# A Fourier mixing layer and an MLP on one core: first batch in units of four frequencies by whole filter rows, its last stages in residue order and mostly inside the MLP

## The chip, the cores and the metric

The kernel runs on one core of a Trainium2 chip. The metric is the device time of one execution in microseconds (us). A run's time is a little longer than the span of its profile (784.55 against 782.8 us for the kernel before), because the span counts from the first to the last instruction. Nearly all numbers below are read from profiles, so they are spans and moments within them; whole times and ratios are marked as such. In the profiles PE is TensorE, which does the matmuls and transposes; DVE (VectorE), ACT (ScalarE) and POOL (GpSimd) do the copies and products; SP issues DMAs. PSUM is the memory that the matmuls here write to and that DVE and ACT copy from.

## The reference

```python
def _attn_ref(x, filt_r, filt_i):            # x: 8 x 3008 x 256
    X = np.fft.rfft(x, axis=1)
    Y = X * (filt_r + 1j * filt_i)[None]     # filters: 1505 x 256
    return np.fft.irfft(Y, n=x.shape[1], axis=1).astype(np.float32)

def _moe_ref(x, w_in, w_out, beta):          # x: 24064 x 256, w_in: 256 x 2048
    h = x @ w_in
    g = h * (1.0 / (1.0 + np.exp(-beta * h)))
    return (g @ w_out).astype(np.float32)    # w_out: 2048 x 256
```

The MLP takes the 8 x 3008 tokens of the mixing layer. It is by far the larger part: 752 steps of two matmuls of 512 columns (into `hps`) and four of 256 columns (into `acc`).

## The kernel before

The length 3008 is split as 47 x 64. The transform is four stages of matmuls: two forward (s1, s2), a product with the filter, two backward (s3, s4). The tables of sines are made on the chip. Batch 0 is done ahead of the MLP, in what I call the head. Batches 1 to 7 are done inside the MLP's steps, as TensorE, DVE and ACT allow, by way of two DRAM scratch arrays.

The head as it was (cuts marked `# ...`). The filters are loaded in six parts of 8 frequencies by 128 channels, that is in rows of 512 bytes. `fr` comes into the lower 64 partitions and `fi` into the upper; POOL copies each to the other half (`spread`). DVE makes two products from each part:

```python
parts = ((0, KH, 0, E2), (KH, 2 * KH, 0, E2), (2 * KH, NK, 0, E2), (0, KH, E2, D), ...)
def load_filters(k0, k1, d0, d1):
    for filt, dst, p0 in ((filt_r, fr_sb, 0), (filt_i, fi_sb, M)):
        for q0, off, sg in ((p0, k0, 1), (p0 + H, N1 - k0, -1)):
            src = AP(filt.tensor, filt.offset + off * D + d0, [[N1 * D, H], [sg * D, n], [1, d1 - d0]])
            nc.sync.dma_start(dst[q0 : q0 + H, k0:k1, d0:d1], src)
def spread(n):
    nc.gpsimd.tensor_copy(fr_sb[M:, ks, ds], fr_sb[:M, ks, ds])
    nc.gpsimd.tensor_copy(fi_sb[:M, ks, ds], fi_sb[M:, ks, ds])
def s2_0(n):
    # ... eight matmuls into ps
    for c, filt in enumerate((fr_sb, fi_sb)):
        nc.vector.tensor_tensor(r_t[:], ps[:], filt[:, ks, ds], ALU.mult)      # pq_t
# POOL's order:
spread(0); spread(1); spread(2); spread(3)      # ...
spread(4)
nc.gpsimd.dma_start(win_sb[:], moe_w_in.rearrange("(dc p) f -> p dc f", p=P))
spread(5)
for g in range(4):
    load_x(1, g)                                 # x of batch 1
```

The end of the head: the result `zT` is turned by 64 transposes into `zz0` (z_turn), and 64 residue matmuls (f_0 and s4_0) make `y`. Much of the first half of the channels is done while the second half's products are still being made:

```python
s3_0(3); s2_0(5); f_0(0, 0, True); z_turn(0, 2, True); f_0(0, 1, True); z_turn(0, 3, True)
s3_0(4); s3_0(5, (False, True)); z_turn(1, 0, False, True); z_turn(1, 1, True, True)  # ...
f_0(0, 7, False); s4_0(1, 3, False)
```

The MLP loop, the plan of batch 1 (the numbers are MLP steps) and the last block. The `lags` say how many steps later the four output matmuls of a step come:

```python
for s in range(NSTEP + 4):
    # two matmuls hps <- win_sb, y ; ACT: gT <- silu(hps)
    for fn, a in plan.get(s, ()): fn(*a)        # stages of the next batch
    # four matmuls acc <- gT, wout_sb of an earlier step; DVE copies acc to ost at a block's end
s1_steps(1, range(16), [o + i // 2 for i in range(16)], False, range(1, 16, 2))
s23_steps(1, [o + r for r in (19, 21, 23, 26, 28, 30, 34, 36, 39, 41, 44, 46)], 5, 1)
lags[NBLK - 1] = (2, 2, 5, 7)
```

## Time and profile before

| | before |
|---|---|
| time, median of 3 runs | 784.76 us (784.7 to 784.91) |
| span of the profile | 782.8 us |
| first hps matmul of the MLP | 41.54 us |
| last filter product ends | 32.77 us |
| start of first hps to start of last matmul | 736.9 us |
| start of last matmul to the end | 4.29 us |

First the windows view of the kernel before. Its columns are the stretch, its length, then busy time and number of instructions of PE, PE's weight loads, DVE, ACT and POOL, the granted clock, the DMA share and GB/s.

```profile
core 0: us, PE busy (x) PEld busy (x) DVE busy (x) ACT busy (x) POOL busy (x), PEclk, DMA share, GB/s
0.00:41.54 41.54, 32.41 (x438) 25.09 (x440) 32.89 (x56) 30.32 (x43) 27.59 (x46) 1.00 1.04 203
41.54:778.50 736.96, 731.53 (x5540) 519.83 (x5632) 404.50 (x626) 528.18 (x781) 124.02 (x114) 1.00 0.39 108
```

In the head no engine is full and the DMA engines are (share 1.04). In the MLP TensorE is busy nearly all the time, and its starts follow at a fixed pitch: 109 ns for 256 columns, 216 ns for 512, 55 ns for a transpose of 128, about 42 ns for 94.

Next POOL's and DVE's timelines of the kernel before, at the end of the filter work (start, busy time, engine, line, what).

```profile
25.51 1.04 POOL L468 COPY fi_sb<-fi_sb 64x1024 f32<-64x1024 f32 x1
26.50 0.84 POOL L513 DMA_DIRECT2D win_sb<-in_moe_w_in_dram  x1
27.39 1.03 POOL L467 COPY fr_sb<-fr_sb 64x1024 f32<-64x1024 f32 x1
28.48 1.04 POOL L468 COPY fi_sb<-fi_sb 64x1024 f32<-64x1024 f32 x1
...
31.55 1.21 DVE L433 TENSOR_TENSOR pq_t<-sps,fi_sb 128x1024 bf16<-128x1024 f32 x1
```

The last filter copy starts at 28.48 us and does not wait; the product that needs it runs from 31.55. There are two microseconds of slack between them. The w_in load is issued at 26.50 us.

Last the chain of waits of the kernel before, in order of time, around the end of the head.

```profile
32.93 1.02 ACT zz L112
33.95 0.92 ACT zT L112
...
40.00 2.25 DVE y L116 x3
42.26 0.05 issue
42.30 0.39 PE hps L756
```

### The profile page before, as it was taken

The page shows a single profiled execution, that of the slowest core. Times are in us where ns is not written, and L with a number is a line of the kernel's source. Part 1 is how long each engine was busy: PE and PEld are TensorE (multiplying, and loading weights), DVE is VectorE, ACT ScalarE, POOL GpSimd, SP SyncE. Part 2 cuts the span into 40 slices and gives each one's busy share as a digit, 9 for nine tenths or more (in the row PEclk, how much of TensorE's full clock was granted, in tenths as well). Part 3 has the DMA queues.
Part 4 walks back from the last instruction along what each step waited for, and adds up shares of the span by engine and source line. Part 5 has one row for each costly group of instructions (what it writes and reads, how often), then busy time and mean ns, then how long its engine had stood idle before and what let it go on. Part 6 is the DMA issues. An engine that isn't in the chain of part 4 may idle for free.

```text
span 782.8 us, 15166 instructions
## 1 busy us (share of the span) xinstructions
PE 764.2 (98%) x5978; PEld 544.9 (70%) x6071; DVE 438.1 (56%) x682; ACT 558.5 (71%) x824; POOL 151.6 (19%) x160
## 2 busy tenths in 40 slices
PE   8799999999999999999999999999999999999997
PEld 5666767766677667866678666786667776676665
DVE  7747654776556665566655675466655666320101
ACT  6788867676667766776667776677666777777776
POOL 6714300322012120122101222012200222000000
PEclk9999999999999999999999999999999999999999
DMA  9966675234822349033580416612164211500101
GB/s 178 230 190 138 145 201 167 68 88 120 238 75 64 98 114 260 32 84 99 121 236 29 126 56 158 198 58 85 49 188 118 66 48 49 155 28 28 55 28 55
DMA packets 89835, 88.51 MB, mean 113 GB/s; under 512 B 5708, under 2 KB 80972, under 8 KB 89764
## 3 DMA queue, kind: packets, MB, share of 16 engines
q1 hardware_dynamic: 85588, 73.81, 31.8%
q0 software_dynamic: 4032, 13.60, 10.5%
q8 instruction: 47, 0.77, 0.4%
q14 instruction: 24, 0.20, 0.1%
q10 hardware_dynamic: 144, 0.13, 0.1%
HBM read 54.47 MB, written 46.66 MB: 129 GB/s over the span
## 4 chain that ended last, share of the span: by engine, by line
PE 94%; ACT 2%; issue 1%; DVE 0%; ACTq 0%
PE acc L774 43%; PE hps L756 39%; PE ps L572 3%; PE ps L639 3%; PE ps L617 3%; PE ps L588 2%; ACT zT L112 1%; ACT zz L112 1%; ACT t3s L291 0%; DVE y L116 0%; PE sps L396 0%; PE sps L444 0%; PE tps L396 0%; ACT a L112 0%; PE sps L428 0%
## 5 line engine op out<-in xcount | busy, mean ns | idle before, releaser
L765 ACT ACTIVATE gT<-hps,beta_sb 128x512 bf16<-128x512 f32 x752 | 515.8, 687 | 208.3 <-PE hps L756 187.2
L774 PE MATMUL acc<-wout_sb,gT 128*128 128x256 bf16 x3008 | 453.2, 272 | 2.5
L756 PE MATMUL hps<-y,win_sb 128*128 128x512 bf16 (+7 forms) x1636 | 428.3, 350 | 1.1 <-ACT y L112 0.6
L774 PEld LDWEIGHTS <-gT 128*128 128x128 bf16 x3008 | 287.6, 98 | 125.9 <-issue 1.2
L607 POOL TENSOR_TENSOR yh<-a_t,b_t 128x512 bf16<-128x512 f32 x84 | 106.4, 1266 | 420.4 <-DVE b_t L606 419.5
L756 PEld LDWEIGHTS <-win_sb 128*128 128x128 bf16 x1728 | 164.9, 98 | 25.6 <-issue 0.7
L114 DVE COPY ost<-acc 128x512 f32<-128x512 f32 (+1 forms) x94 | 60.0, 679 | 147.1 <-PE acc L774 147.1
L114 DVE CAST a<-ps 96x512 bf16<-96x512 f32 x104 | 70.9, 685 | 52.1 <-PE ps L572 48.0
L602 DVE TENSOR_TENSOR a_t<-ps,fr_sb 128x512 f32<-128x512 f32 x84 | 58.1, 692 | 70.0 <-PE ps L588 69.5
L116 DVE TENSOR_SCALAR y<-ps 128x376 bf16<-128x376 f32 x104 | 56.0, 548 | 59.3 <-PE ps L639 59.1
L603 DVE SCALAR_TENSOR_TENSOR b_t<-ps,fi_sb 64x512 f32<-64x512 f32 x84 | 58.2, 692 | 1.1
L606 DVE TENSOR_TENSOR b_t<-ps,fi_sb 64x512 f32<-64x512 f32 x84 | 57.4, 683 | 1.1
L114 DVE CAST z<-ps 128x512 bf16<-128x512 f32 x72 | 49.3, 684 | 1.7 <-PE ps L617 0.8
L639 PEld LDWEIGHTS <-zz 96*128 96x128 bf16 x448 | 29.8, 98 | 22.9
L572 PE MATMUL ps<-xg,t 94*96 94x512 bf16 x112 | 41.5, 381 | 0.6
L639 PE MATMUL ps<-t,zz 96*128 96x94 bf16 x448 | 34.7, 205 | 0.8
L617 PE MATMUL ps<-yh,t 128*128 128x256 bf16 x168 | 32.1, 273 | 0.6
L588 PE MATMUL ps<-a,t 128*128 128x256 bf16 x168 | 32.1, 273 | 0.3
L617 PEld LDWEIGHTS <-t 128*128 128x128 bf16 x168 | 16.3, 98 | 17.7
L588 PEld LDWEIGHTS <-t 128*128 128x128 bf16 x168 | 16.1, 98 | 15.2
L171 POOL DMA_DIRECT2D xg<-in_x_dram x24 | 12.4, 519 | 56.5 <-PE ps L572 56.5
L572 PEld LDWEIGHTS <-t 94*96 94x96 bf16 x112 | 13.8, 123 | 10.3
(103 smaller groups left out, 185.9 us busy)
## 6 DMA issues: line engine op xcount, KB each, us to landing
out_dram<-ost SPq DMA_DIRECT2D x46, 512.0 KB, 3.0
d<-a SPq DMA_DIRECT2D x28, 384.0 KB, 4.7
a<-d SPq DMA_DIRECT2D x28, 384.0 KB, 5.1
d<-z SPq DMA_DIRECT2D x28, 384.0 KB, 3.7
zz<-d SPq DMA_DIRECT2D x28, 384.0 KB, 6.1
xg<-in_x_dram POOLq DMA_DIRECT2D x24, 384.0 KB, 6.2
ws<-in_moe_w_out_dram SPq DMA_DIRECT2D x4, 512.0 KB, 6.0
fr_sb<-in_filt_r_dram SPq DMA_DIRECT2D x12, 128.0 KB, 4.6
```

The source lines that it names most:

```text
L114: nc.vector.tensor_copy(dst, src)
L572: nc.tensor.matmul(ps[:KP], lhsT=t1[:], rhs=xg[b, g][:NP, jj : jj + 2, :], start=True, stop=True)
L588: nc.tensor.matmul(ps[:, e, :], lhsT=t2[:, k0 + e, :], rhs=st["a2", b, g][:, kk + e, :], start=True, stop=True,)
L602: nc.vector.tensor_tensor(a_t[:], ps[:], fr_sb[:, ks, :], ALU.mult)
L603: nc.vector.scalar_tensor_tensor(b_t[:M], ps[M:], -1.0, fi_sb[M:, ks, :], ALU.mult, ALU.mult)
L606: nc.vector.tensor_tensor(b_t[M:], ps[:M], fi_sb[M:, ks, :], ALU.mult)
L607: nc.gpsimd.tensor_tensor(yh[:], a_t[:], b_t[:], ALU.add)
L617: nc.tensor.matmul(ps[:, e, :], lhsT=t3[:, 2 * i + e, :], rhs=yh[:, e, :], start=True, stop=True)
L639: nc.tensor.matmul(ps[:, e, :NP], lhsT=zz[:, j0 % JG + e, dc * P : (dc + 1) * P], rhs=t4[:], start=True, stop=True,)
L756: nc.tensor.matmul(hps[:, pos - t0 : pos - t0 + ln], lhsT=win_sb[:, dc, fb * P : (fb + 1) * P], rhs=ys[b][:, dc, n0 : n0 + ln], start=(dc ...
L765: nc.scalar.activation(gT[:], hps[:], ACT.Silu, scale=beta_sb[:, fb : fb + 1])
L774: nc.tensor.matmul(acc_of(i, tb)[:, tb % 2, :], lhsT=blk[i * NFB + fb][:, tb * P : (tb + 1) * P], rhs=wout_sb[:, fb, :], start=(fb == 0 an ...
```

## The change

The intent is to shorten the head. The head is worked in six units of four frequencies by all 256 channels, so the filters come in whole rows of 1 KB, and where four rows lie together, in 4 KB. The sign of the second table goes into the product, so that two half tables less have to be made. The tokens of batch 0 are ordered by residue, so that the first MLP block needs only one quarter of the transposes and residue matmuls; the other three quarters, 48 transposes and 48 matmuls, go into MLP steps 0 to 23. The core of the diff:

```diff
-    parts = ((0, KH, 0, E2), (KH, 2 * KH, 0, E2), ...)
+    def load_filters(k0, k1):        # rows of [1, D] instead of [1, d1 - d0]
...
+        nc.vector.scalar_tensor_tensor(
+            pq[u, 1][:], ps[:], rot[:], fi_sb[:, ks, :], ALU.mult, ALU.mult
+        )
...
-    spread(3)                        # POOL's order before: spread 0 to 4, w_in, spread 5, x
+    for u in range(3):
+        spread(u)
+    nc.gpsimd.dma_start(win_sb[:], moe_w_in.rearrange("(dc p) f -> p dc f", p=P))
+    spread(3)
+    spread(4)
+    load_x(1, 0)
+    spread(5)
+    for g in range(1, 4):
+        load_x(1, g)
...
+    s5 = [lps.tile([P, KU, P], F32, name="lp", tag="lp") for _ in range(NDC)]
+    s3_0(NUN - 1, s5)                # the last unit, then only quarter 0:
+    # ... z_evac, z_turn(0, ...), f4(0, ...), f4_head, f4_tail
...
+            at(0, z_late, 1, 0)
+            at(1, z_late, 1, 1)
+            s1_steps(1, range(16), [(2 * i + 1) // 3 for i in range(16)], False, (1, 4, 7, 10, 13))
+            for i, r in enumerate((11, 11, 12, 13)):
+                at(r, f_late, 1, i // 2, i % 2)
+            # ... quarters 2 and 3 in steps 13 to 23
-            s23_steps(1, [o + r for r in (19, 21, 23, 26, 28, 30, 34, 36, 39, 41, 44, 46)], 5, 1)
+            s23_steps(1, [o + r for r in (21, 23, 26, 28, 30, 32, 35, 37, 39, 41, 44, 46)], 5, 1)
...
-    lags[NBLK - 1] = (2, 2, 5, 7)
+    lags[NBLK - 1] = (2, 2, 4, 6)
```

## The prediction

> **What bounds the kernel now.** The span is 782.8 us. The timeline shows two regimes. From the first MLP matmul (hps, 41.54 us) on, TensorE hardly waits after two steps: the windows show 99.3 us busy in each 100, and starts follow at a fixed pitch: 109 ns for 256 columns, 216 for 512, 55 for a 128-column transpose, about 42 for 94 columns. (The Trainium skill, "TensorE: Matmul & The Clock Gate", section "Wait — 56ns, not 53.3ns?", gives 56 ns between 128-column matmuls; this trace agrees, with 55.) Before 41.54 us TensorE has slack: busy 7.2 to 8.0 of 10 us between 10 and 40 us. There the pace is set by a chain: POOL's filter copies (2.1 us a unit, first at 13.76 us, waiting for the filter DMA), twelve DVE filter products (1.22 us each, one per 1.14 us, 16.5 to 32.8 us, nearly gapless), then last unit, transposes to zz, 64 residue matmuls and their copies by ACT and DVE, 32.8 to 42.3 us.
>
> **What the change does.** It adds no matmul work; it cuts the 8.8 us tail between the last product and the first MLP step. Only the first quarter (16 transposes, 16 residue matmuls) stays ahead of the MLP; 48 transposes and 48 matmuls go into MLP steps 0 to 23. The filters arrive in 1 KB packets instead of 512 B; the packets' times (about 48 against 41 ns, so about 340 against 220 GB/s) put the six units earlier.
>
> **Costing the head.** POOL: spread from about 13.2 us, six units at 2.2 us plus 1.4 us of DMA issues: last unit ready at 27.7. DVE: first product at about 15.8 (16.5 before), so the last ends at about 30.0 to 30.5 (32.8 before). The tail is then one chain of short steps with a hop each: 0.5 us matmuls, 0.3 and 0.5 z copies, 0.5 transposes, 0.4 to 0.6 zz copies, 0.2 matmuls, two rounds of 0.4 y copies: about 3.3 us. First MLP matmul at about 33.8 us, 7.7 us earlier. win_sb, issued at about 20 instead of 26.5 and 8.9 us to landing, should be there at about 30.
>
> **Costing the MLP.** TensorE is the bound there, so what moves in is paid in full: 48 x 55 ns + 48 x 42 ns = 4.65 us. DVE gets 6 x 0.61 + 12 x 0.56 = 10.4 us more over 24 steps; it is 60 to 70% busy, so little stalls. I add 0.7 us for the opening, where leftover y copies, z copies and batch-1 copies meet on DVE. Batch 1's DRAM round trip (about 8 us) still fits before step 21.
>
> Net: -7.7 + 4.65 + 0.7 = -2.35 us, from 784.76 to about **782.4 us**; 8 in 10 between 780.0 and 784.7. Chances: faster by over 2% 0.01, within 2% 0.98, slower 0.01.
>
> **What would show the steps.** Right: the first hps matmul near 33.8 us; the last filter product ending near 30; POOL's first copy near 13; TensorE time from first hps to the end about 5 us longer than 740.5; 1 KB filter packets. Wrong: DVE gaps before products (POOL or ACT late), TensorE waits for win_sb, for wout_sb, or for fpsum buffers in steps 0 to 23, or a2 landing after step 21.
>
> **What would make it wrong.** (1) The head doesn't shorten because POOL's spread, gated by DMA, or ACT's in-order queue holds the products. (2) win_sb lands late because filters, w_out and x compete. (3) DVE's burst at steps 11 to 24 stalls TensorE.

## The result, and the profile after

The changed kernel took 787.53 us (median of 4 runs, 786.97 to 788.13) against 784.73 us (4 runs, 784.48 to 784.91). The ratio is 1.0036 with a 95% interval of 1.0019 to 1.0053. Ratios here are the mean time of one kernel's fast runs over that of the other's in the same rounds, so not quite the ratio of the medians. The change made the kernel slower by about 2.8 us; I had predicted 2.35 us faster, and the measured time lies outside my range.

| | before | predicted | after |
|---|---|---|---|
| last filter product ends | 32.77 | 30.0 to 30.5 | 33.34 |
| first hps matmul | 41.54 | 33.8 | 36.84 |
| first hps to last matmul | 736.9 | + 5.35 | 743.3 (+ 6.4) |
| last matmul to the end | 4.29 | same | 5.02 (+ 0.7) |
| span | 782.8 | 780.4 | 785.2 |

The miss of 4.8 us in the span is thus 3.0 us of head, 1.0 us of MLP and 0.7 us after the last matmul. The windows view of the changed kernel, with the columns as before:

```profile
0.00:36.84 36.84, 28.68 (x318) 20.76 (x319) 28.69 (x50) 24.50 (x35) 24.66 (x39) 0.97 0.98 211
36.84:780.20 743.36, 741.72 (x5730) 524.28 (x5728) 417.31 (x663) 528.41 (x779) 125.81 (x115) 1.00 0.40 108
```

The head is 4.7 us shorter, the MLP 6.4 us longer. The granted clock of the head is no longer 1.00 (0.97 on average); I return to that. POOL's timeline of the changed kernel, at the end of the filter work:

```profile
21.13 0.84 POOL L477 DMA_DIRECT2D win_sb<-in_moe_w_in_dram  x1
...
26.87 1.04 POOL L472 COPY fr_sb<-fr_sb 64x1024 f32<-64x1024 f32 x1
30.99 1.04 POOL L473 COPY fi_sb<-fi_sb 64x1024 f32<-64x1024 f32 x1 [3.08 <-DMA fi_sb<-in_filt_i_dram]
```

POOL waited 3.08 us for the last load of `fi`. The chain of waits of the changed kernel, in order of time, says where that load was:

```profile
17.80 4.45 DMA fi_sb<-in_filt_i_dram
22.25 0.02 issue
22.26 8.61 DMA fi_sb<-in_filt_i_dram
...
30.99 1.05 POOL fi_sb L473
32.03 0.02 issue
32.06 1.30 DVE pq_t L435
```

The last load of `fi`, 128 KB, took 8.61 us from issue to landing; a load of the same size ahead of it in this chain took 4.45. TensorE's timeline of the changed kernel shows what it cost:

```profile
29.83 0.62 PE L444 MATMUL lp<-t,pq_t 128*128 128x128 bf16 x8
33.40 0.62 PE L444 MATMUL lp<-t,pq_t 128*128 128x128 bf16 x8 [2.95 <-DVE pq_t L435]
34.17 1.58 PE L400 MATMUL zp<-ident,y 128*128 128x128 bf16 x16
35.54 1.46 PE L405 MATMUL fp<-t,zz 96*128 96x94 bf16 x16
36.84 1.21 PE L763 MATMUL hps<-y,win_sb 128*128 128x512 bf16 x2
```

In the new order nothing else is left to do: TensorE waits 2.95 us. Sixteen transposes, which took 1.07 us in the kernel before, then take 1.58 us.

Inside the MLP two waits are new. TensorE's and DVE's timelines of the changed kernel around them:

```profile
66.23 0.39 PE L570 MATMUL ps<-a,t 128*128 128x256 bf16 x2 [0.42 <-DVE b_t L588]
...
76.20 0.69 DVE L584 TENSOR_TENSOR a_t<-ps,fr_sb 128x512 f32<-128x512 f32 x1
76.91 0.69 DVE L585 SCALAR_TENSOR_TENSOR b_t<-ps,fi_sb 64x512 f32<-64x512 f32 x1
77.61 0.69 DVE L588 TENSOR_TENSOR b_t<-ps,fi_sb 64x512 f32<-64x512 f32 x1
78.33 1.29 DVE L112 COPY ost<-acc 128x512 f32<-128x512 f32 x2
...
79.07 0.38 PE L781 MATMUL acc<-wout_sb,gT 128*128 128x256 bf16 x2 [0.93 <-DVE ost L112]
```

Measured from start to start and less the usual pitch they are 0.58 and 1.09 us. At the first, a matmul of batch 1's second stage waits for a PSUM buffer whose products queue on DVE behind the moved residue copies. At the second, in step 34, the accumulators of a block are copied out late, because the filter product of step 32 stands before the copy: three DVE instructions from 76.20 to 78.30 us, behind those of steps 28 and 30 with no pause. The old plan had no product between steps 30 and 34; there DVE was free at 75.89 us and waited for the accumulators until 76.81.

### The profile page after: what moved, and what is told of

It reads as the page before. It is cut to its first block, busy times and chain, and to the rows that moved or that the text cites. A ratio compares the mean times of both kernels' runs of the same rounds, so it can differ in the third digit from the quotient of the medians.

```text
span 785.2 us, 15235 instructions
## 1 busy us (share of the span) xinstructions
PE 770.6 (98%) x6046; PEld 545.0 (69%) x6046; DVE 446.7 (57%) x713; ACT 553.1 (70%) x814; POOL 150.5 (19%) x154
## 4 chain that ended last, share of the span: by engine, by line
PE 93%; DVE 2%; DMA 2%; SPq 0%; ACT 0%; issue 0%; POOL 0%; DVEq 0%; POOLq 0%; ACTq 0%
PE acc L781 41%; PE hps L763 41%; PE ps L554 3%; PE ps L622 2%; DMA fi_sb<-in_filt_i_dram 2%; PE ps L600 2%; PE ps L570 2%; DVE b_t L585 0%; DVE a_t L584 0%; SPq L91 0%; DVE b_t L588 0%; PE tp L400 0%; PE ps L405 0%; DVE u L224 0%; PE zp L400 0%
## 5 line engine op out<-in xcount | busy, mean ns | idle before, releaser
L763 PE MATMUL hps<-y,win_sb 128*128 128x512 bf16 (+7 forms) x1728 | 448.6, 352 | 0.2 <-ACT y L110 0.2
L112 DVE CAST a<-ps 96x512 bf16<-96x512 f32 x107 | 72.8, 685 | 52.0 <-PE ps L554 47.9
L114 DVE TENSOR_SCALAR y<-ps 128x376 bf16<-128x376 f32 (+2 forms) x128 | 63.2, 511 | 62.0 <-PE ps L622 59.0
```

The source lines that it names most:

```text
L112: nc.vector.tensor_copy(dst, src)
L114: nc.vector.tensor_scalar_mul(dst, src, scale)
L763: nc.tensor.matmul(hps[:, pos - t0 : pos - t0 + ln], lhsT=win_sb[:, dc, fb * P : (fb + 1) * P], rhs=ys[b][:, dc, n0 : n0 + ln], start=(dc ...
```

## The experiments

Each experiment is one edit of the changed kernel or of the kernel before. The changed kernel itself was timed earlier, so I compare the ratios to the kernel before (1.0036 for the changed kernel), or moments in the profiles. All outputs were correct.

### Who held up the last filter load?

The theory (C) is that the w_in load crowds it out. The Trainium skill, "DMA: Bandwidth & Descriptors", section "Queues, rings and completion order", says that each DMA engine goes round-robin between its queues, a whole packet at a time. In the packet records of the trace a packet of the w_in load (issued by POOL, converted to bf16) took 324 ns and the 1 KB packets of filters and w_out 46 to 75 ns. If the engines alternate, a queue of small packets gets a small part of the time. The DMA view of the changed kernel from 26 to 29 us, when the filter queue (q1) sent the 1 KB packets of the last `fi` load, shows it (packets, MB, share of the engines' time; q0 carries w_in):

```profile
q0 software_dynamic: 132, 0.54, 89.3%
q1 hardware_dynamic: 119, 0.12, 14.7%
```

The two queues took turns nearly one for one. Turns are not all of it: from 24.93 to 26.12 us the filter queue moved no data at all and w_in ran alone, which I can't explain. The change moved the w_in load from 26.5 to 21.1 us, into the filter stream. The rivals are the w_out loads, which follow the filters in the same queue, and the new shape of the filter loads.

**a_winlate**: w_in after the fifth unit (the first x load moves too, to after the sixth).

```diff
-    nc.gpsimd.dma_start(win_sb[:], ...)
     spread(3)
     spread(4)
-    load_x(1, 0)
+    nc.gpsimd.dma_start(win_sb[:], ...)
     spread(5)
+    load_x(1, 0)
```

> The changed kernel with one thing moved: the w_in load is issued on the POOL queue after the fifth filter unit has been spread (about 26 us) instead of after the third (21.1 us), and the first x load of batch 1 after the sixth. Theory C (crowding): the last fi load landed at 30.9 us because its 1 KB packets (46 to 75 ns) shared the DMA engines with the 4 KB packets (324 ns) of the w_in load. Then the last fi unit lands by about 26 us, POOL's last fi copy starts near 28 instead of 30.99, the last filter product ends near 31 instead of 33.3, w_in lands at about 33 to 35, the first hps matmul starts at 34 to 35.5 us instead of 36.84, and the time falls by 1.3 to 2.8 us. Rival theory W: the w_out loads or the new shape of the filter loads themselves hold the last unit back: then it still lands near 30 us and the time does not fall, or rises as w_in comes later.

Measured: 785.22 us (5 runs, 784.8 to 785.34), ratio 1.0005 (0.9991 to 1.0018). That is 0.31% or about 2.4 us better than the changed kernel. POOL's, DVE's and TensorE's timelines of this run:

```profile
25.82 0.84 POOL L479 DMA_DIRECT2D win_sb<-in_moe_w_in_dram  x1
26.71 1.03 POOL L472 COPY fr_sb<-fr_sb 64x1024 f32<-64x1024 f32 x1
27.80 1.04 POOL L473 COPY fi_sb<-fi_sb 64x1024 f32<-64x1024 f32 x1
29.68 1.27 DVE L435 SCALAR_TENSOR_TENSOR pq_t<-sps,rot,fi_sb 128x1024 bf16<-128x1024 f32 x1
34.78 0.61 PE L763 MATMUL hps<-y,win_sb 128*128 128x512 bf16 x2 [0.87 <-DMA win_sb<-in_moe_w_in_dram]
```

The last copy starts at 27.80 us with no wait, the last product ends at 30.96, and the first hps matmul comes at 34.78, now after a wait for w_in. Theory C holds. My reckoning of the head's filter work was nearly right for this order, not for the one that the change has: the last unit was ready at 28.84 us (predicted 27.7), and the last product, which DVE's own pace then set, ended 0.5 us after the predicted 30.0 to 30.5. A second new wait, of 0.96 us, stands in step 0, for the first x load of batch 1, which landed at 36.58 us behind w_in (34.73).

**a_wsgp**: the w_out loads taken out of the filters' queue.

```diff
-        nc.sync.dma_start(
+        (nc.gpsimd if f0 < 2 * WG else nc.sync).dma_start(
             ws[:], moe_w_out[...])
```

> The changed kernel with the first two w_out loads taken from the SP queue and issued on the POOL queue after the x loads of batch 1, so that nothing follows the filter loads in their own queue. Theory C (the w_in load crowds out the last filter load): POOL's last fi copy still starts near 30 to 31 us. Rival W (the w_out loads crowd it): it starts near 28 us. The total says nothing here, since w_out comes later than the first output matmul needs it, 1 to 5 us of TensorE wait in MLP step 2.

Measured: one run, 790.49 us, with a 2.2 us wait of TensorE for w_out as foreseen. The last fi copy started at 31.48 us. The w_out loads are not the cause.

**b_winearly**: the kernel before with w_in issued after the third part.

```diff
     spread(2)
+    nc.gpsimd.dma_start(win_sb[:], ...)
     spread(3)
...
-    nc.gpsimd.dma_start(win_sb[:], ...)      # was between spread(4) and spread(5)
```

> The kernel before, with the w_in load alone issued earlier: after the third filter unit (about 21 us) instead of after the fifth (26.5 us). Theory C: in the kernel before too the last fi load then lands at about 29 to 31 us, its POOL copy starts there instead of at 28.5, the last product ends near 34 to 35 instead of 32.8, and the time rises by 1 to 2.5 us. Rival W (only the new whole-row filter loads suffer, or w_out does it): the last fi copy stays near 28 to 29 us and the time stays within 0.4 us.

Measured: 785.09 us (4 runs, of which one took 788.22), ratio 1.0014 (0.9997 to 1.0031). So a rise of the time by 1 to 2.5 us, as expected, is not shown. POOL's, DVE's and TensorE's timelines, then the DMA view from 26 to 29 us:

```profile
27.38 1.04 POOL L467 COPY fr_sb<-fr_sb 64x1024 f32<-64x1024 f32 x1
33.35 1.04 POOL L468 COPY fi_sb<-fi_sb 64x1024 f32<-64x1024 f32 x1 [4.93 <-DMA fi_sb<-in_filt_i_dram]
34.42 1.23 DVE L433 TENSOR_TENSOR pq_t<-sps,fi_sb 128x1024 bf16<-128x1024 f32 x1 [2.92 <-POOL fi_sb L468]
42.13 0.38 PE L756 MATMUL hps<-y,win_sb 128*128 128x512 bf16 x1 [0.43 <-ACT y L112]
...
q0 software_dynamic: 136, 0.56, 92.0%
q1 hardware_dynamic: 136, 0.07, 11.5%
```

With the old filter loads the last part is held up too, by 4.93 us, more than I expected; so the new shape is not the cause. The turns are again one for one, and with packets of 512 bytes the filters got only 0.07 MB in these 3 us, against 0.12 MB with 1 KB. As only the w_in load was moved here, the x load is not needed to explain the delay. The last product ends at 35.64 instead of 32.77 us, but the first hps matmul comes only 0.6 us later (42.13 against 41.54). The old head hides 2.3 of 2.9 us, as ACT's copies of the first half of the channels stand in the same stretch. In the changed kernel the same delay is paid in full.

### Are the two MLP waits DVE's order?

**a_sched**: only the steps of batch 1's second stage.

```diff
-s23_steps(1, [o + r for r in (21, 23, 26, 28, 30, 32, 35, 37, 39, 41, 44, 46)], 5, 1)
+s23_steps(1, [o + r for r in (22, 25, 27, 29, 31, 35, 37, 39, 41, 43, 45, 47)], 5, 1)
```

> The changed kernel with only the steps of batch 1's second stage moved: 22, 25, 27, 29, 31, 35, 37, 39, 41, 43, 45, 47 instead of 21, 23, 26, 28, 30, 32, 35, 37, 39, 41, 44, 46. Theory D: the two TensorE waits of 0.58 us (near 65.6 us, a PSUM buffer held by the filter products while the moved residue copies queue on DVE) and 1.09 us (near 77.9 us, the output copy of a block behind three products in a row) come from DVE's order, so both vanish and the time falls by 1.2 to 1.7 us. Rival: DVE is simply too full in steps 21 to 48, the waits move elsewhere and the time stays within 0.4 us.

Measured: 785.09 us (5 runs, 784.0 to 786.09), ratio 1.0005 (0.9992 to 1.0017). Both waits are gone and none has come in their place. TensorE's and DVE's timelines, at the end of the head and at the block's copy:

```profile
33.06 0.62 PE L444 MATMUL lp<-t,pq_t 128*128 128x128 bf16 x8 [2.61 <-DVE pq_t L435]
35.95 0.86 PE L763 MATMUL hps<-y,win_sb 128*128 128x512 bf16 x2
...
75.17 1.29 DVE L112 COPY ost<-acc 128x512 f32<-128x512 f32 x2
```

The MLP of the profile takes 741.2 instead of 743.3 us, of which the two waits are 1.67; most of the rest lies before the first output matmul (3.55 instead of 3.91 us), where the changed kernel ran in part at half clock. The time fell by about 2.4 us, more than the 1.2 to 1.7 expected, but the intervals are wide (0.13 and 0.17%), and this profile, unlike that of the changed kernel, shows no fall of the clock, which I turn to now.

### What did the fall of the clock cost?

The granted clock of the changed kernel's profile is 1.0 but for one stretch of 3413 ns from 34.54 us, where it is 0.5. The windows view, cut at the edges of that stretch:

```profile
31.13:34.54 3.41, 0.99 (x15) 1.00 1.09 299
34.54:37.96 3.42, 3.38 (x33) 0.50 1.07 212
```

In the window ahead of it TensorE was busy for 0.99 of 3.41 us, because of the wait for the last product. The Trainium skill, "TensorE: Matmul & The Clock Gate", section "What's actually happening", describes a free-running window of 3413 ns by whose activity the clock is set to full or half; the trace agrees in length and level. The stretch at half clock covers the transposes, the residue matmuls and the first hps matmuls. All four runs of the changed kernel have a mean clock of 0.996 to 0.998, which is one to two such stretches (half of 3.41 us is 0.2% of the span); most runs of the kernel before have 1.0.

**a_spin**: dummy matmuls in the wait, into a bank of the pool that the residue matmuls use.

```diff
         for c in range(2):
+            if c == 1 and u == NUN - 1:
+                fill = fps.tile([P, 4, P], F32, name="fp", tag="fp")
+                for _ in range(9):
+                    nc.tensor.matmul(fill..., lhsT=rest[:, :P], rhs=rest[:], start=True, stop=True)
             src = pq.pop((u, c))
```

> The changed kernel with nine dummy matmuls of 512 columns (about 1.9 us) put into the 2.95 us in which TensorE waits for the last filter product. The last filter unit still lands late (near 31 us). Theory H: that wait empties most of one clock window, and the granted clock then falls to 0.5 for 3.4 us (34.5 to 38.0 us in the profile), just when the tail and the first MLP matmuls run; with the dummy work the clock stays at 1.0, the first hps matmul follows the last product by about 2.9 us instead of 3.5, and the time falls by 0.6 to 1.7 us with a smaller spread from run to run. Rival: the dip has no weight, as the tail is a chain of ACT and DVE copies; the time stays within 0.4 us.

Measured: 790.12 us, ratio 1.0067. The experiment failed: the bank takes over memory of the pool that the last product still reads, so the dummy matmuls waited for that very product (from 33.72 us on) and then stood in the way of the real ones. The first hps matmul came at 39.90 us.

**a_spin2**: the dummy matmuls on a free bank, ahead of the last unit's first eight matmuls.

```diff
     unit(4)
+    fill = tpsum.tile([P, 512], F32, name="tps", tag="tps")
+    for _ in range(10):
+        nc.tensor.matmul(fill[:], lhsT=rest[:, :P], rhs=rest[:], start=True, stop=True)
     banks.close()
```

> The changed kernel with ten dummy matmuls of 512 columns (about 2.2 us), this time on a PSUM bank that nothing waits for and ahead of the last unit's first eight matmuls, so that they end before the last filter product does (about 33.3 us). Theory H: the granted clock then stays at 1.0 through the tail in most runs, the first hps matmul follows the last product by about 2.9 us instead of 3.5, and the time falls by 0.6 to 1.7 us with a smaller spread. Rival: the dip of the clock has no weight; the time stays within 0.4 us of the changed kernel's 787.5.

Measured: 786.64 us (5 runs, 786.23 to 787.75), ratio 1.0024 (1.0010 to 1.0038) against 1.0036 (1.0019 to 1.0053). The mean clocks of the runs are 0.998, 0.999, 0.999, 1.000 and 1.000, and the two runs at 1.000 took 786.64 and 786.23. The profile fell on the run at 0.998, and shows the fall again. The dummy work fell into the window before the one that decided, as the windows view shows:

```profile
28.73:32.15 3.42, 3.37 (x32) 1.00 1.05 252
32.15:35.56 3.41, 1.53 (x25) 1.00 1.07 290
35.56:38.97 3.41, 3.37 (x32) 0.50 1.07 214
```

The fall costs something near 0.9 us by the ratios, in the range that I gave, but the intervals overlap. The profiles agree: from the last product to the first hps it was 2.94 us in the three with neither fall nor wait for w_in (a_sched, a_best, a_best2), and 3.28 to 4.02 us in the five of the same tail with the fall in this stretch (the changed kernel 3.50, a_spin2 3.28, a_lag 3.60, a_dup 3.88, a_wsgp 4.02). I call a cost shown in the tail; what it is in the whole time is not shown to the tenth. In all profiles, six windows between the first rise to full clock and 760 us had less than 1 us of TensorE work (0.00 to 0.99 us), and a fall followed each; of nine windows with 1.53 to 1.88 us, a fall followed two (1.53 and 1.83). In a_sched the same late filter left 1.54 and 1.63 us, as the wait lay across the edge of two windows, and no fall came: where the edge lies is chance. A few matmul records can be missing from a trace, so these shares are rough, and no threshold can be read from them.

### What did the move into the MLP gain?

**a_dup**: each of the 48 moved transposes done twice.

```diff
-            nc.tensor.transpose(tp[:w, i, :], zT[:, e, j * KP : j * KP + w], ident[:])
+            for _ in range(2 if n == JG else 1):
+                nc.tensor.transpose(tp[:w, i, :], zT[:, e, j * KP : j * KP + w], ident[:])
```

> The changed kernel with each of the 48 transposes that were moved into the MLP done twice (the second writes the same values over the first; the result is right). Theory P: TensorE is the bound in the MLP, so moved work is paid in full: MLP time from the first hps matmul to the last matmul grows by 48 x 55 ns = 2.6 us, and so does the total, give or take 0.5. Rival: TensorE has slack in these 24 steps, and the total grows by less than 1 us.

Measured: 789.77 us (5 runs), ratio 1.0059 (1.0045 to 1.0073), which is 0.23% or 1.8 us over the changed kernel: less than the 2.1 us that I had allowed at least, but by the two intervals it could be anything from about 0 to 3.5. The profile says more. Its MLP takes 745.6 us, 2.25 more, for 2.64 us of added TensorE work; and the changed kernel's MLP began at half clock, at a cost of some 0.4 us (3.91 against 3.55 us to the first output matmul in a_sched), while a_dup's began after the fall. So work that goes into the MLP is paid there, nearly in full.

**a_head**: the move alone undone.

```diff
-    late = []                              # one quarter, then f4_tail
+    for hh in range(HB):                   # all four quarters in the head
+        # ... z_turn(hh + 1, ...), then f4, f4_head and f4_tail of hh, on DVE and ACT in turn
...
-            at(0, z_late, 1, 0)            # and all other z_late and f_late steps
```

> The changed kernel with the 48 transposes, 48 residue matmuls and their copies put back ahead of the MLP (order of tokens and all else as changed). Theory P: the move only shifts work from a stretch that ACT and DVE pace to one that TensorE paces. Then the first hps matmul comes 5 to 6 us later (about 2 us of copies per engine for each of three quarters), the MLP gets 4.7 us of TensorE work and the 0.58 us wait shorter, and the time changes by less than 1.5 us either way. Rival: the copies hide well in the MLP and the move is worth 3 us or more; then the time rises by at least that.

Measured: 788.46 us (5 runs, 787.41 to 789.19), ratio 1.0046 (1.0033 to 1.0058). The first hps matmul comes at 42.99 us, 6.1 later; the MLP takes 737.5 us, 5.8 less. So the move gives back nearly all that it takes from the head. By the ratios it is worth about 0.8 us of time, but the intervals overlap almost wholly (about -1 to +2.5 us); the rival's 3 us are ruled out, a gain is not shown.

### The stretch after the last matmul

**a_lag** puts the lags back, **b_lag** gives them to the kernel before.

```diff
# a_lag
-    lags[NBLK - 1] = (2, 2, 4, 6)
+    lags[NBLK - 1] = (2, 2, 5, 7)
# b_lag
-    lags[NBLK - 1] = (2, 2, 5, 7)
+    lags[NBLK - 1] = (2, 2, 4, 6)
```

> The changed kernel with only the lags of the last block put back to (2, 2, 5, 7) from (2, 2, 4, 6). Theory L: the shorter lags bring the last three output writes closer together, which made the stretch from the last matmul's start to the end 5.02 us long instead of 4.29; put back it is 4.2 to 4.4 us and the time falls by 0.6 to 0.8 us. Rival: the stretch differs by chance of the write's completion or through something set up earlier in the program; then it stays at 4.9 to 5.1 us and the time is unchanged.

> The kernel before with only the lags of the last block changed as the change has them. The lags put back gave 0.22 us of the 0.72 us by which the stretch after the last matmul grew. If the lags alone matter in the kernel before too, the stretch grows from 4.29 to about 4.5 us here; if it grows to 5.0, the lags were the whole cause and something else kept it long in the run that put them back.

Measured: a_lag 787.49 us (5 runs), ratio 1.0035, so no change in the time that these runs could show; the stretch is 4.79 us instead of 5.02. b_lag (one run, 784.40 us): 4.52 instead of 4.29 us. The lags are 0.23 us of the 0.72, in both directions. The other 0.5 us is not the lags, against my expectation. The last write is issued 0.83 us after the start of the last matmul in a_lag and 0.76 in the kernel before, and its sixteen completions come between 2.90 and 3.58 us in the one, 2.79 and 2.96 in the other. Only the last of the sixteen is late: the fifteenth came at 3.08 us in a_lag. The traces show what goes with it. In all twelve profiles of kernels with the new structure, one 8 KB packet of the instruction queue (q14) starts 2.3 to 2.9 us after the last matmul's start, while the write is in flight, and the sixteenth completion is 0.22 to 0.53 us behind the fifteenth; in the three of the old structure the packet starts at 4.0 to 4.2 us, after the last completion, and the gap is at most 0.04 us. No run moved that packet, so a cause is not shown.

### A version that beats both

**a_all**: a_winlate, a_sched and a_lag together (their three diffs).

> The changed kernel with the three repairs together: w_in issued after the fifth filter unit, the second-stage steps of batch 1 spaced as in the run that removed the waits, the old lags. If the three causes are separate, their gains add: in the profile 1.7 + 2.1 + 0.7 us, so a span near 780.7 us against 785.2 of the changed kernel, and a time 1 to 2.5 us under the kernel before on the same chip. If they share a cause, the gain stays under 3 us.

Measured: 785.15 us (5 runs, 783.46 to 786.51), ratio 1.0003 (0.9991 to 1.0016). The gains did not add. The first hps matmul comes at 34.61 us, but the x load and w_in landed at 36.53 and 34.56, TensorE waited 1.08 and 0.39 us in the first steps, and then the clock fell (from 36.9 us for one window; mean clocks 0.995 to 0.999). With the filters out of the way the DMA stream itself is the limit: once one load is early, the next in the stream decides.

**a_best**: in addition w_in by halves.

```diff
-    nc.gpsimd.dma_start(win_sb[:], moe_w_in...)
+    nc.gpsimd.dma_start(win_sb[:, :, :FH], win_v[:, :, :FH])
     spread(5)
     load_x(1, 0)
+    nc.gpsimd.dma_start(win_sb[:, :, FH:], win_v[:, :, FH:])
```

> As the three repairs together, and the w_in load split by columns: the half that MLP steps 0 to 7 need is issued after the fifth filter unit, then the first x load of batch 1, then the second half. If landing of w_in (34.73 us in the run that moved it) and of x (36.58 us, a 0.96 us TensorE wait) still gate the start, both land about 2.5 us earlier, the first hps matmul starts near 34.3 us, the wait before the first batch-1 matmul is gone, and the time falls by a further 0.5 to 1.5 us below the three repairs. If the last filter product (30.96 us) and the tail of 3.4 us gate it, only the 0.96 us wait goes.

Measured: 782.53 us (5 runs, 781.97 to 783.59), ratio 0.9973 (0.9960 to 0.9985). The first half of w_in landed at 32.17 us and x at 34.03. The first hps matmul comes at 33.91, and the clock is 0.999 to 1.000 in all runs. A wait of 0.61 us for the second x load remains at 38.3 us.

**a_best2**: the second half of w_in after the second x load, and batch 1's first stage one step later.

```diff
     load_x(1, 0)
-    nc.gpsimd.dma_start(win_sb[:, :, FH:], win_v[:, :, FH:])
...
-    for g in range(1, 4):
+    load_x(1, 1)
+    nc.gpsimd.dma_start(win_sb[:, :, FH:], win_v[:, :, FH:])
+    for g in range(2, 4):
         load_x(1, g)
...
-            s1_steps(1, range(16), [(2 * i + 1) // 3 for i in range(16)], ...)
+            s1_steps(1, range(16), [(2 * i + 4) // 3 for i in range(16)], ...)
```

> The best version so far (three repairs and the split w_in load) with the second half of w_in issued after the second x load of batch 1 instead of after the first, and batch 1's first stage one step later. It should take away the 0.61 us wait for x in MLP step 3 to 4, so the time falls by 0.3 to 0.8 us, to about 782.0; if the second half of w_in then comes too late for step 8 (about 43 us), a wait for it appears there instead and nothing is gained.

Measured: 781.97 us (5 runs, 781.42 to 782.48), ratio 0.9963 (0.9949 to 0.9976). The wait is gone but for 0.10 us, and no wait for w_in has come. This is 2.5 us under the kernel before in the same call (784.44) and about 5.7 us under the changed kernel by the ratios. The step over a_best (0.1%) is within the intervals.

## Why the prediction was wrong

- **What bounds the kernel before, and that moved work is paid in full: right.** From the first hps matmul to the last the MLP grew by 6.4 us; 48 x 55 ns + 48 x 42 ns = 4.65 us of it is the moved work by the prediction's sum. In a_sched, without the two waits and the fall of the clock, it grew by 4.3. a_dup and a_head agree with the principle.
- **"last unit ready at 27.7" and "the last ends at about 30.0 to 30.5": this is the step that failed.** The last unit was ready at 32.03 us and its product ended at 33.34. I had costed POOL's and DVE's work (nearly right: 28.84 and 30.96 us in a_winlate), and I had noted that w_in goes out at about 20 us instead of 26.5, but only as a gain for w_in. I didn't ask what the earlier load collides with. It crowded the last filter load, which took 8.61 instead of 4.45 us. My list of dangers had the gate ("POOL's spread, gated by DMA"), with no size and no weight in the estimate; and where I did name the competition of loads, w_in was to be the loser, but w_in landed at 31.22 us and nothing waited for it. The last product ended 2.8 us after the predicted 30.5, which is most of the 3.0 us by which the first hps matmul missed 33.8 us: 2.4 of it is the late load (33.34 against 30.96 in a_winlate), about 0.5 that the products took longer than I had costed.
- **"about 340 against 220 GB/s ... put the six units earlier": wrong.** With no w_in in the way (a_winlate) the last filter byte landed at 27.03 us, against 27.39 in the kernel before. I took the rate of packets of w_out for that of a stream of filters. The Trainium skill, "DMA: Bandwidth & Descriptors", section "Specifications", gives 512 bytes as the least transfer for line rate, so this figure promised nothing for going from 512 bytes to 1 KB; the runs agree.
- **"about 3.3 us" of tail: nearly right**, 3.50 us in the profile with half the clock in most of it, 2.94 in a_sched without. I had not foreseen the fall of the clock. It comes with the wait for the last filter when that wait lies within one window (0.99 us of work left in the changed kernel); in a_sched it did not come.
- **"I add 0.7 us for the opening" and "so little stalls": wrong place.** To the first output matmul the change added 0.69 us, but 0.46 of that is moved work set against fewer s1 matmuls, so 0.23 us are stalls and half clock. The loss came later, 0.58 and 1.09 us in steps 23 and 34, from DVE's order and not from its load; a_sched took both away at the same load.
- **The end of the kernel**, which I took as unchanged, grew by 0.72 us: 0.23 from the lags; the other 0.5 goes with one late completion of the last write, its cause open.

In sum: 3.0 us (late filter and clock) + 1.0 us (MLP) + 0.7 us (end) = 4.8 us between the predicted and the measured change of the span, from -2.35 to +2.4.

## What to carry to other kernels

When a change issues a load earlier, ask which loads are in flight at that moment, and which of them the critical path needs first: an early load with large packets can double the time of the small one that everything waits for. A head that keeps independent work beside its last step hides such a delay; one that is cut to a single chain pays for it in full, and TensorE's idle time can then cost clock on top. Moving work from a stretch that is not TensorE's limit into one that is gains only the difference (here a gain that the runs can't tell from nothing, from a head that got 6.1 us shorter).

## What the Trainium skill lacked or had wrong

- "TensorE: Matmul & The Clock Gate", section "What's actually happening", names an idle window as what brings the clock down. Here windows that were partly busy did: 0.99 of 3.41 us in the changed kernel, 1.53 us in a_spin2 and 1.83 us in a_all. Seven others with 1.54 to 1.88 us did not. The page gives no share at which a window counts as idle, and these runs give no clean one.
- "DMA: Bandwidth & Descriptors", section "Queues, rings and completion order", tells of the round-robin by packets, but not what it can do to the lesser queue: a 128 KB filter load took 8.61 instead of 4.45 us beside a converting load with packets of 324 ns, against its own of 46 to 75 ns, and in b_winearly POOL waited 4.93 us for it.
- No page that I read has a late completion of a write beside a packet of the instruction queue: 3.58 us after the last matmul's start in a_lag, with the packet at 2.29 us, against 2.96 us in the kernel before, with the packet at 3.98 us. It goes with the 0.5 us left open.
